# Seeds of a convolution kernel: the factors of the powers as products on GpSimd instead of VectorE

## The chip, the core and the metric

The kernel runs on one core of a Trainium2 chip. A core has TensorE (PE; weight loads are listed apart as PEld), VectorE (DVE), ScalarE (ACT), GpSimd (POOL) and SyncE (SP), which issues the DMAs. Each engine works through its own list of instructions in order; semaphores tie the lists together. The metric is the device time of one execution in microseconds (us); smaller is better.

## The reference, cut to what matters

Two independent halves are computed from fp32 inputs and concatenated: a long convolution (S4D) and an attention with 16 heads.

```python
def _A_ref(u, log_A_real, A_imag, C_real, C_imag, log_dt, D_skip):   # L = 2048, D = 448, N = 256
    dt = jnp.exp(log_dt)
    A = -jnp.exp(log_A_real) + 1j * A_imag
    C = (C_real + 1j * C_imag) * dt[:, None]
    P = jnp.exp((A * dt[:, None])[:, :, None] * pos[None, None, :])
    K = 2.0 * jnp.einsum("dn,dnl->dl", C, P).real
    ...                                     # y = u convolved with K (by FFT of length 2 L)
    return y + u * D_skip[None, None, :]

def _B_ref(x, wqkv, wo):                    # S = 2048, D = 448, H = 16, Dh = 28
    ...                                     # q, k, v = heads of x @ wqkv
    p = _softmax(jnp.einsum("bhqd,bhkd->bhqk", q, k) * Dh ** -0.5, axis=-1)
    return einsum("bhqk,bhkd->bhqd", p, v) ... @ wo
```

## The kernel before

The kernel has two phases.

**The projection phase** (the first 260 us or so) does two things side by side. For the attention it projects x: the 2048 rows come in four chunks `c` of 512. `transposes(c)` turns a chunk on TensorE into four PSUM tiles `pt`, which ScalarE rounds into `xh` and DVE subtracts into the low half `xl`. `qk_proj(c, s, g)` then makes a PSUM tile `pm` for K (s = 1) or Q (s = 0) of a group g of four heads from 12 matrix products, and its `evac` splits it: ScalarE writes the high half of `hl`, DVE the low half (and a difference `kb` for c < 2), and SP sends `hl` to memory as `k` or `q`. `v_proj` makes V (`vst`). There are three `pm` tiles, so PE can start a job only when the job three before it is evacuated. K and Q are read back as `khat` and `qhat` before the attention begins; the chunk c = 3 projects V first and then K and Q.

For the convolution, `seeds(o)` makes the starting values for the powers of exp(A dt), for eight groups `o` of 56 channels, in thirteen steps: scale and turn the parameters (`nat`, `pn`, `tr`), phases and their reduction (tile `tri`, three parts `r`, `sn`, `mg` of 128 x 11 x 112, one for each power of two), sines on ScalarE, `sizes` (Exp of `mg`, whose argument is a product of `tr` with `pw` on GpSimd), and then the products of sizes and sines:

- `g_base` on GpSimd: `gz`, and `r` at two powers in place (listed as `tri<-tri` 128x224);
- `factors` (the change): for three powers at a time, `mg*r` and `mg*sn` into the part `zz` of the tile `sg`, then negative copies by ScalarE (`sg<-sg`). It is called as `fa` and `fb`, two products of 128x336 each, so four for a group;
- `e_base` on GpSimd: six products 128x112 into the tile `qhat` (its place serves as the seeds' e tile), listed as `qhat<-tri`;
- `e3` on DVE: the third power from these (`qhat<-qhat`, `px<-qhat`, `qhat<-qhat,px`);
- `e5` on GpSimd: six operations of 128x336 (`qhat<-qhat`, `x_e<-qhat`, `qhat<-qhat,x_e`);
- `g_first` on DVE: the first powers of g (`sg`, `px`), then copies by ScalarE.

`sg` and the e tile go to memory (`sd`). The tiles `tri` and `sg` have two buffers, the e tile three.

The steps of the seeds and the jobs of the projection are written out in slots: four slots for each group, with the jobs spread over 37 slots. In this phase the order that results on each engine is not the program's: the tile framework's scheduler places the instructions when the kernel is built. Where two engines are called with the same step, the order therefore can change in other places as well.

At the end of the phase the row maxima of the first block are taken (DVE reads `pm` and `pt`).

**The attention phase** keeps the program's order on every engine: for 256 steps, scores (`pss`), Exp on ScalarE (`p`), the product with V (`po`), and between them the maxima of later blocks, the powers of the convolution (`e` on GpSimd, `g` on DVE), its transforms and the output.

All instructions are recorded with the line of one helper (L75), so they are told apart by their tiles.

Of the kernel before, what the change touches and what calls it, by code (L numbers as in the profile page):

```python
# [90 lines left out]
def body(ctx, tc, a, out):  # L91
# [120 lines left out]
    with ExitStack() as st:  # L212
# [98 lines left out]
        mul = lambda e, o_, x_, y_: e.tensor_tensor(o_, x_, y_, ALU.mult)  # L311

        def seeds(o):

            q = {}
            vec, pol, act = nc.vector, nc.gpsimd, nc.scalar
# [3 lines left out]
            vk = lambda t, k: t[:, k:k + 3, :].rearrange("p k (b h) -> p k b h", h=16)  # L320
# [79 lines left out]

            def factors(i, k, p_, n_):
                zz, mg = q["zz"], q["mg"]
                mul(vec, zz[:, i:i + 3, :, 0, :], vk(mg, k), vk(q["r"], k))
                mul(vec, zz[:, i:i + 3, :, p_, :], vk(mg, k), vk(q["sn"], k))
                for k in range(i, i + 3):
                    act.activation(zz[:, k, :, n_, :], zz[:, k, :, p_, :], AF.Copy, scale=-1.0)

# [19 lines left out]
            def load():  # L427
                if o not in nats:
                    load_nat(o)
                q["nat"] = nats.pop(o)  # L430
            dts = lambda *r: [lambda i=i: times_dt(i) for i in r]
            fa, fb = lambda: factors(0, 3, 2, 1), lambda: factors(3, 8, 1, 2)
            return [[load], [exp_a] + dts(1, 2, 3), dts(0), [turn], [phases], [reduce], [sines], [sizes, g_base],
                    [places, fa, e_base], [e3, g_first], [fb, e5, g_copies], [put_g], [put_e]]
# [695 lines left out]
```

## Time and profile before

| | us |
|---|---|
| three runs before | 1300.53, 1301.88, 1303.57 |
| median of the runs | 1301.88 |
| profiled execution, span from first to last instruction | 1301.1 |

A time of the profiled execution beyond its span is not given; the runs lie 0.6 below to 2.5 above that span, and their median 0.8 above it.

| engine | busy us | share of the span |
|---|---|---|
| PE | 1228.2 | 94% |
| ACT | 952.4 | 73% |
| DVE | 948.0 | 73% |
| POOL | 871.1 | 67% |

The profile is one execution. An instruction's row has its start, its duration, engine, operation, output and inputs with their shapes, and in brackets how long the engine stood idle before it and which instruction ended that wait. Idle time of an engine that is not on the way to the end costs nothing. A duration includes time in which the instruction had begun but was held up.

### The profile page before, as it was taken

Reading aid. Unit: us, or ns where it says so; the run is one execution under the profiler, and the core shown is the slowest. Engines: PE = TensorE matmul, PEld = TensorE weight load, DVE = VectorE, ACT = ScalarE, POOL = GpSimd, SP = SyncE. Lnnn points to the kernel's source line nnn. Section 1 sums busy time; section 2 is a strip of 40 time slices with the busy share of each in tenths; the row PEclk is TensorE's granted clock in tenths of the full one; section 3 lists DMA queues with packets and bytes.
Section 4 is the critical chain, followed back from the end, with each engine's and each line's share of the span. In section 5 each row is a group of like instructions: output and inputs, shape, how many; then the busy total and the mean of one; then the engine's idle time right before and its main releaser. Section 6 shows DMA issues by size and latency. Waiting matters only on the chain.

```text
span 1301.1 us, 33177 instructions
## 1 busy us (share of the span) xinstructions
PE 1228.2 (94%) x12625; PEld 701.0 (54%) x12625; DVE 948.0 (73%) x2106; ACT 952.4 (73%) x2068; POOL 871.1 (67%) x736
## 2 busy tenths in 40 slices
PE   6878985899999999999999999999999999999997
PEld 5657763355555555555555555555555555544433
DVE  5887896987777887787788888888888655645111
ACT  4775763488888888888888888888887766756552
POOL 3676683298888878888869999998996212424421
PEclk9888997999999999999999999999999999999999
DMA  6677769835866555458644131733425453647656
GB/s 194 203 258 244 249 206 294 237 77 124 195 137 149 124 146 148 140 147 231 181 126 96 54 95 32 182 91 83 103 51 148 153 158 133 201 144 244 198 162 174
DMA packets 200088, 205.35 MB, mean 158 GB/s; under 512 B 95993, under 2 KB 158521, under 8 KB 197881
## 3 DMA queue, kind: packets, MB, share of 16 engines
q1 hardware_dynamic: 199928, 203.23, 56.2%
q8 instruction: 100, 1.64, 0.5%
q14 instruction: 60, 0.48, 0.1%
HBM read 120.73 MB, written 82.18 MB: 156 GB/s over the span
## 4 chain that ended last, share of the span: by engine, by line
PE 71%; DVE 10%; DMA 6%; POOL 5%; ACT 3%; issue 3%; SPq 0%; POOLq 0%; ACTq 0%; DVEq 0%
PE pm L75 40%; PE pss L75 16%; PE po L75 15%; DVE tri L75 2%; DVE mx L75 2%; POOL e L75 1%; POOL qhat L75 1%; DMA k<-hl 1%; ACT tri L75 1%; DVE qhat L75 1%; DVE sg L75 1%; DMA tri<-in_B_wqkv 1%; DVE px L75 1%; DMA khat<-k 1%; DMA ut<-in_A_u 1%
## 5 line engine op out<-in xcount | busy, mean ns | idle before, releaser
L75 ACT ACTIVATE p<-pss 128x512 f32<-128x512 f32 x1024 | 560.9, 609 | 111.6 <-PE pss L75 108.6
L75 PE MATMUL pss<-qhat,khat 128*128 128x512 f32 x1024 | 402.5, 399 | 1.5 <-ACT p L75 1.4
L75 DVE TENSOR_REDUCE mx<-pm 128x1 f32<-128x512 f32 x500 | 321.4, 684 | 109.2 <-PE pm L75 107.1
L75 PE MATMUL pm<-khat,qhat 128*128 128x512 f32 x749 | 326.3, 438 | 3.4 <-DVE mx L75 2.1
L75 POOL TENSOR_TENSOR e<-e,sdb 128x256 f32<-128x256 f32 x168 | 202.0, 1202 | 116.2 <-ACT e L75 61.2
L75 PE MATMUL po<-p,v 128*32 128x512 f32 x2048 | 269.1, 594 | 0.0
L75 POOL TENSOR_TENSOR e<-e,eu 128x256 f32<-128x256 f32 x168 | 248.4, 1478 | 13.2
L75 PEld LDWEIGHTS pm<-khat,qhat 128*128 128x128 f32 x749 | 141.0, 189 | 199.7 <-ACT p L75 47.8
L75 DVE CUSTOM_DVE_ANT_0 rl<-pm,rl 128x512 f32<-128x512 f32 x249 | 171.4, 688 | 65.2 <-ACT rl L75 61.5
L75 PEld LDWEIGHTS pss<-qhat,khat 128*128 128x128 f32 x1024 | 190.2, 188 | 45.7 <-issue 10.8
L75 POOL TENSOR_TENSOR eu<-e,sdb 128x256 f32<-128x256 f32 x168 | 202.2, 1203 | 0.0
L75 POOL TENSOR_TENSOR p<-pr,pr 64x448 f32<-64x448 f32 x64 | 73.3, 1145 | 158.5 <-PE pm L75 133.2
L75 ACT ACTIVATE rl<-pm 128x512 f32<-128x512 f32 x249 | 150.8, 606 | 20.4 <-PE pm L75 20.4
L75 DVE TENSOR_TENSOR g<-g,zg 128x128 f32<-128x128 f32 x392 | 162.1, 413 | 3.4
L75 PE MATMUL pm<-xh,khat 112*128 112x512 f32 x256 | 94.1, 451 | 23.2 <-DVE hl L75 11.1
L75 PE MATMUL pm<-kdif,qhat 128*128 128x512 f32 x249 | 100.5, 404 | 2.6 <-DMA v<-v 1.3
L75 DVE TENSOR_TENSOR zg<-g,zg 128x128 f32<-128x128 f32 x224 | 88.0, 393 | 5.0
L75 PEld LDWEIGHTS pm<-e,g 128*32 128x32 f32 x3584 | 57.2, 109 | 43.8 <-issue 16.1
L75 DVE TENSOR_TENSOR pr<-pm,ub 128x448 f32<-128x448 f32 x64 | 37.0, 619 | 56.4 <-PE pm L75 42.0
L75 PEld LDWEIGHTS pm<-xh,khat 112*128 112x128 f32 x256 | 54.2, 217 | 39.4 <-DVE hl L75 12.9
L75 PE MATMUL pm<-e,g 128*32 128x64 f32 x3584 | 73.0, 222 | 1.9 <-POOL e L75 1.9
L75 ACT ACTIVATE y<-pm 128x448 f32<-128x448 f32 x48 | 26.5, 553 | 58.2 <-PE pm L75 33.8
(134 smaller groups left out, 1470.3 us busy)
## 6 DMA issues: line engine op xcount, KB each, us to landing
sdb<-sd SPq DMA_DIRECT2D x56, 336.0 KB
khat<-k SPq DMA_DIRECT2D x64, 256.0 KB
qhat<-q SPq DMA_DIRECT2D x64, 256.0 KB
sd<-sg SPq DMA_DIRECT2D x8, 1456.0 KB
k<-hl SPq DMA_DIRECT2D x16, 512.0 KB
q<-hl SPq DMA_DIRECT2D x16, 512.0 KB
mw<-in_mw SPq DMA_DIRECT2D x16, 512.0 KB
sd<-qhat SPq DMA_DIRECT2D x8, 896.0 KB
```

The lines of the kernel that those rows point to most:

```text
L75: i = f(*args, **kw)
```

## The change

The two products of `factors` are issued to GpSimd instead of DVE. Thus 32 products of 128x336 (four for each of eight groups) change the engine; the operands, the copies on ScalarE that follow, and all else in the source stay the same. The order in which the scheduler places the other instructions of the projection phase changes in some places.

```diff
             def factors(i, k, p_, n_):
                 zz, mg = q["zz"], q["mg"]
-                mul(vec, zz[:, i:i + 3, :, 0, :], vk(mg, k), vk(q["r"], k))
-                mul(vec, zz[:, i:i + 3, :, p_, :], vk(mg, k), vk(q["sn"], k))
+                mul(pol, zz[:, i:i + 3, :, 0, :], vk(mg, k), vk(q["r"], k))
+                mul(pol, zz[:, i:i + 3, :, p_, :], vk(mg, k), vk(q["sn"], k))
                 for k in range(i, i + 3):
                     act.activation(zz[:, k, :, n_, :], zz[:, k, :, p_, :], AF.Copy, scale=-1.0)
```

In the changed order of group 2 and 3 (found from the two programs' lists), GpSimd has group 2's four products between group 2's bases, and three of group 3's before the second half of group 3's bases; group 3's `gz` now comes before those bases and no longer after them. DVE has the first `xl` of c = 2, and ScalarE the second `xh`, behind all of group 3's `g_first`; before, five operations of `g_first` came after the first `xl`. On DVE, group 2's first `sg<-pn,tri` (a step of `g_first`) now stands ahead of the evacuation `hl` of the next K job; before, it stood behind two evacuations. At the end of the phase the order of SP's DMAs is the same but for single places.

## The prediction

> **What bounds the kernel now.** I read the page, then the busy time by stretch, the waits of TensorE, the chain that ended last, and last how the change reorders the instructions of each engine.
>
> ```profile
> span 1301.1 us, 33177 instructions
> ```
> ```profile
> 30.00:212.00 182.00, 144.04 (x628) 115.87 (x628) 149.98 (x249) 125.19 (x250) 126.42 (x137) 0.88 0.71 237
> 212.00:238.00 26.00, 20.18 (x49) 10.06 (x49) 21.38 (x48) 7.77 (x13) 0.00 (x0) 0.84 1.05 266
> 262.00:1301.00 1039.00, 1022.95 (x11806) 550.18 (x11804) 740.31 (x1720) 794.34 (x1756) 727.70 (x571) 1.00 0.52 138
> ```
> After each stretch and its length stand the busy us of PE, PEld, DVE, ACT and POOL, the granted clock, the DMA share and GB/s. From 262 us PE is busy for 98.5% of the time, and nothing there is changed: that part moves as a whole. The moved products lie in 30 to 212 us, where no engine is full: PE 144 of 182, DVE 150, POOL 126. Waits set its length.
>
> ```profile
> PE pm L75 <- DVE hl L75: 13.2, 6, 5.4
> PE pm L75 <- DVE kb L75: 6.8, 4, 4.3
> PE pt L75 <- DVE xl L75: 6.1, 4, 2.8
> PE pm L75 <- ACT vst L75: 2.8, 1, 2.8
> ```
> ```profile
> 201.61 6.66 DMA q<-hl
> 208.33 12.53 DMA k<-hl
> 220.88 10.06 DMA khat<-k
> ```
> The first fence has what TensorE waited for in that stretch (total, times, longest): 26.1 us (13.2 + 6.8 + 6.1) for evacuations of PSUM on DVE. The second is the chain behind it: the last K and Q go to memory and come back, with the DMA engines full (share 1.05). So a delay of the last evacuations reaches the end nearly one for one, and DVE's queue is what TensorE waits for. That speaks for relieving DVE; the question is what DVE's queue itself waits for.
>
> **The moved instructions.** 32 products 128x336, four for each group o of the seeds.
>
> ```profile
> L75 DVE TENSOR_TENSOR sg<-tri 128x336 f32<-128x336 f32 x32 | 21.7, 684 | 6.3 <-ACT tri L75 6.1
> ```
> ```profile
> L75 DVE TENSOR_TENSOR sg<-tri x32: 490/510/1171, 39.1 to 196.7; 128x336 f32<-128x336 f32 x32
> L75 POOL TENSOR_TENSOR qhat<-tri x48: 418/434/1624, 40.1 to 198.7; 128x112 f32<-128x112 f32 x48
> L75 POOL TENSOR_TENSOR x_e<-qhat x16: 1016/1022/2220, 52.8 to 205.6; 128x336 f32<-128x336 f32 x16
> L75 POOL TENSOR_TENSOR tri<-tr,pw x8: 2244/2249/3445, 31.1 to 181.4; 128x1232 f32<-128x1232 f32 x8
> ```
> The last rows give shortest, median and longest ns. DVE loses 21.7 us (32 x 684 ns). No row shows this product on POOL. The same size there (x_e) takes 1.02 us; a line through 112 and 1232 elements (434 and 2249 ns) gives 0.80 us at 336. I take 1.02, the row of the same size and kind, with 0.80 and, for neighbours' waits, 1.3 as ends (684/510 = 1.34 is how far waiting stretched the same products on DVE). POOL gains 33 us (26 to 42) and stands at 159 of 182 us (152 to 168). The table of the Trainium skill, GPSIMD Engine Reference, 3.1 Elementwise, has POOL 1.96 times slower than DVE for this operation; as an estimate from 490 ns that is 0.96 us, and the sum below would be 0.5 us smaller. No DMA is moved.
>
> **Where it lands.** A mean of 159 hides the dense places.
>
> ```profile
> 77.00:118.00 41.00, 27.77 (x104) 22.38 (x103) 36.47 (x60) 29.74 (x63) 32.08 (x36) 0.79 0.62 215
> 118.00:160.00 42.00, 38.81 (x187) 31.53 (x185) 32.14 (x48) 28.82 (x52) 21.92 (x28) 0.96 0.76 255
> 160.00:208.00 48.00, 36.46 (x146) 28.85 (x145) 39.68 (x70) 29.19 (x60) 39.31 (x39) 0.88 0.74 232
> ```
> In 77 to 118 us groups 2 and 3 follow each other without a pause: eight products more make 32.1 + 8.2 = 40.3 of 41 us, so POOL becomes full there, while it still has 20 us idle in the next stretch.
>
> Step 1, Exp behind POOL's product of exponents:
> ```profile
> 77.02 3.44 POOL L75 TENSOR_TENSOR tri<-tr,pw 128x1232 f32<-128x1232 f32 x1
> ...
> 80.50 1.23 ACT L75 ACTIVATE tri<-tri 128x1232 f32<-128x1232 f32 x1 [2.79 <-POOL tri L75]
> ...
> 83.00 1.22 PE L75 MATMUL pm<-xh,khat 112*128 112x512 f32 x2 [5.38 <-DVE hl L75]
> ```
> POOL makes group 2's exponents only after group 1; ACT's Exp waits for them; the next evacuation stands behind Exp in ACT's queue, DVE's half of it behind ACT's, and PE waits 5.38 us. Group 1's last two factor products now come ahead on POOL: 2 x 1.02 = 2.0 us later; its other two fit into waits of POOL.
>
> Step 2, the 3rd power behind POOL's bases:
> ```profile
> 89.69 2.65 POOL L75 TENSOR_TENSOR qhat<-tri 128x112 f32<-128x112 f32 x3
> ...
> 93.03 1.77 POOL L75 TENSOR_TENSOR qhat<-tri 128x112 f32<-128x112 f32 x3
> 95.81 0.81 POOL L75 TENSOR_TENSOR dhl<-kb,dhl 128x256 fp32r<-128x256 f32 x1 [1.01 <-POOL qhat L75]
> 97.26 1.02 POOL L75 TENSOR_TENSOR qhat<-qhat 128x336 f32<-128x336 f32 x1 [0.65 <-DVE qhat L75]
> ...
> 108.44 0.81 POOL L75 TENSOR_TENSOR gz<-tri 128x224 f32<-128x224 f32 x1
> ```
> ```profile
> 107.29 0.58 DVE L75 TENSOR_TENSOR qhat<-qhat 128x112 f32<-128x112 f32 x1 [1.92 <-POOL qhat L75]
> ...
> 113.20 0.68 DVE L75 TENSOR_TENSOR xl<-pt,xh 112x512 fp32r<-112x512 f32 x1
> ...
> 113.94 0.43 PE L75 MATMUL pt<-ident,xn 128*112 128x128 f32 x2 [2.58 <-DVE xl L75]
> ```
> DVE's third power of group 3 already waits 1.92 us for POOL. Behind it in DVE's queue stand the first powers of g and then xl, the low half of the next 512 rows of x, for which PE waits 2.58 us: all of c = 2 hangs on it. In the changed order seven moved products and group 3's gz (0.81) come ahead of those bases: 7 x 1.02 + 0.81 = 7.9 us. Back come about 1.8 us, by which group 2's bases were stretched (2.65 + 1.77 against 6 x 0.434), and 1.7 us of POOL's waits (1.01 + 0.65), which its later work fills. Net 7.9 + 2.0 - 3.5 = 6.4 us.
>
> Step 3: the order also puts xl, and ACT's xh, behind the whole of group 3's first powers; before, five of those operations came after the first xl. The first and the last of the five:
> ```profile
> 114.76 0.39 DVE L75 TENSOR_TENSOR px<-pn,gz 128x224 f32<-128x224 f32 x1
> ...
> 117.82 0.55 DVE L75 TENSOR_TENSOR sg<-sg,px 128x224 f32<-128x224 f32 x1
> ```
> Five at about 0.5 us are 2.5; the moved product that stood ahead of xl is gone (0.7): 1.8 us. The start of c = 2 moves by 6.4 + 1.8 = 8.2 us. By the ends of the product, nine of them (two in step 1, seven in step 2) make it 6.2 at 0.80 and 10.7 at 1.3.
>
> Step 4: from 118 to 160 PE is busy 38.8 of 42 us, so it cannot catch up, while POOL can. In 160 to 208 POOL gets nine products, 9.2 us on 39.3 of 48, and DVE loses nine, 9 x 0.684 = 6.2 us: full against relieved. I take nothing for it, with -6.2 (all of DVE's relief on the path) to +3.4 (39.3 + 9 x 1.3 over 48, and a start without slack) as its ends. The chain of DMAs then follows the last evacuations; one of them already waits for a DMA:
>
> ```profile
> 205.01 0.69 ACT L75 ACTIVATE hl<-pm,kones 128x512 fp32r<-128x512 f32 x1 [5.88 <-DMA k<-hl]
> ```
> That wait could swallow up to 5.9 us of lateness if the DMAs kept their pace, but the DMAs are fed by the same late evacuations, so I take off nothing.
>
> Sum: 1301.1 + 8.2 = 1309.3 us of span. The median of the three runs (1301.9) lies 0.8 above the span: 1310.1, said as 1310.
>
> **Rivals.** *Faster: DVE's relief decides.* TensorE's 26.1 us of waits on DVE shrink with DVE's load, by 21.7 of 150 us or 14%: 3.8 us, 1301.9 - 3.8 = 1298. For it: DVE is the fuller engine and ends most of PE's waits. Against it: at two of the longest, POOL stands behind DVE (steps 1 and 2). It decides if group 3's third power still starts by about 107 us. Chance 0.18.
>
> *The lateness is absorbed.* POOL's waits for ACT's sines are longer than the additions, and the wait of 5.88 us for the DMA takes most of the rest: 8.2 - 5.9 = 2.3, or 1304. Chance 0.12.
>
> *One engine at a time.* Neighbours stretch each other:
>
> ```profile
> 163.88 3.53 POOL L75 TENSOR_TENSOR qhat<-qhat 128x336 f32<-128x336 f32 x1 [0.94 <-DVE tri L75]
> ```
> ```profile
> 164.07 1.44 DVE L75 TENSOR_TENSOR tri<-tri,pw 128x1232 f32<-128x1232 f32 x1
> ```
> A product that takes 1.02 us alone took 3.53 beside DVE's. If one always excludes the other and their common time fills the phase, the moved work costs what it claims: 32 x (1.02 - 0.49) = 17 us, 1301.9 + 17 = 1319. Against it, both still have idle time together in 118 to 160. Chance 0.14. The Trainium skill, SBUF — State Buffer, SBUF: two separate sides, says why: DVE with two inputs in SBUF and a GpSimd instruction take turns on one port pair, for the whole instruction, so these products keep excluding the other engine wherever they run.
>
> **How the numbers follow.** About 0.2% (2.6 us) is what a measurement of this kernel can tell from no change. The forecast (slower, 1306 to 1313) has 0.56, the one-at-a-time rival 0.14: slower 0.70. Absorbed 0.12 counts as the same, relief 0.18 as faster. The range reaches from just under the relief rival, 1297, to the port rival, 1319; it leaves out larger gains, up to DVE's whole 21.7 us, and larger losses.
>
> **What would show it.** In the profile of the changed kernel: the moved product on POOL near 1.02 us (0.80 to 1.3); POOL near 159 us in the phase; the Exp of group 2 starting near 82.5; DVE's third power of group 3 near 113.5, waiting for POOL several us; c = 2's first xl near 121; the chain of DMAs as before, some 8 us later; from there to the end as long as before. A third power near 107 us, or PE's waits on DVE falling below 22 us, would make the forecast wrong.

## The result, and the profile after

The changed kernel is slower: 1316.25 us (median of four runs, 1315.51 to 1316.94). Against the kernel before on the same chip the ratio is 1.0106, with a 95% interval of 1.0087 to 1.0126, or +13.8 us (1% of 1302 us is 13.0 us); the interval is 11.3 to 16.4 us. The forecast was +8.2: the sign and the place were right, the size was too small. The time lies above the 1306 to 1313 that had the largest chance, and below the 1319 of the one-at-a-time rival.

Busy time by stretch in the kernel after, with the columns of the prediction:

```profile
span 1315.2 us, 33183 instructions
```
```profile
77.00:127.00 50.00, 31.22 (x116) 24.82 (x116) 32.54 (x55) 29.95 (x65) 39.51 (x48) 0.79 0.53 182
127.00:170.00 43.00, 38.89 (x180) 31.53 (x178) 26.52 (x39) 26.46 (x46) 22.36 (x29) 0.93 0.73 245
170.00:222.00 52.00, 37.39 (x154) 28.90 (x152) 35.99 (x64) 31.28 (x63) 46.49 (x52) 0.90 0.73 230
276.00:1315.00 1039.00, 1023.11 (x11807) 550.56 (x11806) 741.04 (x1721) 793.86 (x1757) 726.75 (x571) 1.00 0.51 138
```

From 276 us on everything takes 1039 us, as it did from 262 us before: the attention is only 14 us later. All of the loss lies in the projection phase: the stretches of 41, 42 and 48 us are now 50, 43 and 52 us long. The second of these matters, too, because there the forecast took no loss; TensorE's granted clock there (the share of its full clock that the profile shows as granted) is 0.93, where it was 0.96.

What TensorE waited for, from 30 to 225 us (total, times, longest):

```profile
PE pm L75 <- DVE hl L75: 22.7, 7, 6.7
PE pt L75 <- DVE xl L75: 8.5, 5, 2.8
PE pm L75 <- ACT vst L75: 5.3, 3, 3.8
PE pm L75 <- DVE kb L75: 3.0, 3, 1.3
```

The waits on DVE are 34.2 us, after 26.1, although DVE was relieved of 32 products. With ScalarE's part TensorE waited 39.7 us, after 28.9: 10.8 us more, which is most of the loss but not all. TensorE itself also took longer, 146.80 us for 620 matmuls in the phase, where it was 144.04 us for 628 before.

So the question is what DVE did with its time. What DVE waited for from GpSimd in the same stretch, first in the kernel before, then after:

```profile
DVE qhat L75 <- POOL qhat L75: 3.4, 4, 1.9
DVE sg L75 <- POOL tri L75: 2.2, 4, 0.6
DVE px L75 <- POOL qhat L75: 1.4, 3, 0.7
```
```profile
DVE px L75 <- POOL qhat L75: 13.9, 6, 5.1
DVE qhat L75 <- POOL qhat L75: 10.1, 5, 6.4
DVE sg L75 <- POOL tri L75: 7.7, 5, 2.7
```

Before, DVE waited 7.0 us for GpSimd; after, 31.7. The 24.7 us more are about what DVE lost in busy time, 27.9 us (158.35 and 130.46 us in that stretch):

```profile
30.00:225.00 195.00, 153.32 (x651) 121.48 (x651) 158.35 (x268) 128.78 (x256) 126.42 (x137) 0.87 0.74 240
```
```profile
30.00:225.00 195.00, 146.80 (x620) 116.84 (x620) 130.46 (x217) 123.81 (x249) 145.11 (x169) 0.87 0.67 221
```

(Part of the 27.9 is work of the attention that began before 225 us in the kernel before, and not yet in the one after.) DVE gave work away and then stood still for GpSimd's results, ahead of the evacuations that stand behind them in its queue. ScalarE's waits for GpSimd rose in the same way, from 10.8 to 26.0 us.

### The profile page after: what moved, and what is told of

The parts are those of the page before. It is cut to its first block, busy times and chain, and to the rows that moved or that the text cites. A ratio compares the mean times of both kernels' runs of the same rounds, so it can differ in the third digit from the quotient of the medians.

```text
span 1315.2 us, 33183 instructions
## 1 busy us (share of the span) xinstructions
PE 1232.4 (94%) x12625; PEld 703.7 (54%) x12625; DVE 929.6 (71%) x2074; ACT 950.5 (72%) x2068; POOL 889.1 (68%) x768
## 4 chain that ended last, share of the span: by engine, by line
PE 73%; POOL 9%; DVE 7%; ACT 4%; issue 3%; DMA 2%; SPq 1%; POOLq 0%; ACTq 0%; DVEq 0%
PE pm L75 41%; PE pss L75 16%; PE po L75 15%; POOL qhat L75 3%; DVE mx L75 2%; POOL sg L75 2%; POOL e L75 1%; POOL tri L75 1%; DVE rl L75 1%; ACT tri L75 1%; DMA khat<-k 1%; PE pt L75 1%; DVE qhat L75 1%; POOL x_e L75 1%; POOL p L75 1%
## 5 line engine op out<-in xcount | busy, mean ns | idle before, releaser
L75 POOL TENSOR_TENSOR e<-e,eu 128x256 f32<-128x256 f32 x168 | 248.1, 1477 | 13.2
L75 PEld LDWEIGHTS pss<-qhat,khat 128*128 128x128 f32 x1024 | 190.7, 189 | 45.8 <-issue 10.8
L75 PE MATMUL pm<-xh,khat 112*128 112x512 f32 x256 | 93.0, 446 | 21.6 <-DVE hl L75 15.8
```

The lines of the kernel that those rows point to most:

```text
L75: i = f(*args, **kw)
```

## The experiments

Two theories were at stake. **In-order theory:** every engine works strictly in order, so a result that GpSimd makes later also delays all that stands behind its reader on DVE or ScalarE, evacuations above all. **Price theory** (the port rival): each moved product costs the difference of its two durations, or a share of time in which only one of the two engines can work, wherever it stands. Differences in us below are the ratio against the kernel before on the same chip times 1302.

### One pair of groups at a time

Four kernels move only the products of two groups: 0 and 1, 2 and 3, 4 and 5, 6 and 7.

```diff
-                mul(vec, zz[:, i:i + 3, :, 0, :], vk(mg, k), vk(q["r"], k))
-                mul(vec, zz[:, i:i + 3, :, p_, :], vk(mg, k), vk(q["sn"], k))
+                mul(pol if o in (0, 1) else vec, zz[:, i:i + 3, :, 0, :], vk(mg, k), vk(q["r"], k))
+                mul(pol if o in (0, 1) else vec, zz[:, i:i + 3, :, p_, :], vk(mg, k), vk(q["sn"], k))
```

> Only groups 0 and 1 (8 of the 32 products) go to GpSimd. Queue theory (the loss comes where DVE's and ScalarE's queues stand behind GpSimd's bases at two places, group 3 ahead of the next rows of x and group 6 ahead of the first K of c = 3): only step 1's lateness of the Exp of group 2, +1 to +3 us. Port theory (every product costs its extra turn of a port that DVE and GpSimd share, wherever it is moved): 8 x 0.47 = +3.8 us, as the full change's 15 us over 32.

> Only groups 2 and 3 go to GpSimd, the dense place before c = 2. Queue theory: the start of c = 2 comes 6 to 8 us later (DVE's third power of group 3 waits for GpSimd, the low half of x stands behind it), and the end +6 to +8 us, half of the full change's loss with a quarter of the products. Port theory: +3.8 us.

> Only groups 4 and 5 go to GpSimd, where it has waits of 5 to 6 us in each group. Queue theory: the waits take them in, 0 us, from -3 (DVE relieved) to +2. Port theory: +3.8 us.

> Only groups 6 and 7 go to GpSimd. Queue theory: the first evacuation of K of c = 3 stands behind the third power of group 6 in DVE's order and waits for GpSimd: +4 to +6 us, the second part of the full change's loss. Port theory: +3.8 us; this one alone does not tell the two apart, the four together do (even, or 2 / 7 / 0 / 5).

| groups moved | us | ratio, 95% interval | difference, us |
|---|---|---|---|
| 0 and 1 | 1311.13 | 1.0061 (1.0048 to 1.0074) | +7.9 |
| 2 and 3 | 1307.24 | 1.0027 (1.0017 to 1.0037) | +3.5 |
| 4 and 5 | 1303.99 | 1.0001 (0.9992 to 1.0011) | +0.1 |
| 6 and 7 | 1307.03 | 1.0025 (1.0014 to 1.0036) | +3.3 |

The four add up to 14.8, close to the 13.8 of the whole change, but they are far from even. An even price per product is refuted: eight products cost nothing in groups 4 and 5 and 7.9 us in groups 0 and 1. Of my in-order numbers only that for groups 4 and 5 held: I had put most of the loss on groups 2 and 3 (6 to 8 us, 3.5 measured) and 1 to 3 us on groups 0 and 1 (7.9 measured), and 6 and 7 stayed below their 4 to 6. TensorE's waits show the places. The kernel with groups 0 and 1 moved:

```profile
86.14 2.08 PE L75 MATMUL pm<-xh,khat 112*128 112x512 f32 x4 [6.72 <-DVE hl L75]
...
118.78 1.96 PE L75 MATMUL pt<-ident,xn 128*112 128x128 f32 x8 [4.50 <-DVE xl L75]
```
```profile
156.27 0.74 PE L75 MATMUL pm<-vh,xh 112*128 112x448 f32 x1 [4.42 <-ACT vst L75]
```

With groups 4 and 5, and with 6 and 7 moved:

```profile
112.64 1.91 PE L75 MATMUL pt<-ident,xn 128*112 128x128 f32 x8 [2.57 <-DVE xl L75]
```
```profile
191.20 0.92 PE L75 MATMUL pm<-xh,khat 112*128 112x512 f32 x2 [3.98 <-DVE hl L75]
```

Groups 0 and 1 alone bring the lateness of step 1 (83.00 before) and 4.8 us of the 8.5 at the start of c = 2, though none of group 2's or 3's products is moved: the queue of GpSimd hands its lateness from group to group, and DVE's order of this kernel also has `xl` behind more of group 3's `g_first`. Groups 6 and 7 alone make the K evacuation late that step 4 had passed over. Groups 4 and 5 add no such wait of TensorE, and cost nothing. Yet DVE's own waits for GpSimd rise the most there: 15.3 us, against 10.5, 12.6 and 12.2 us in the other three kernels (in the order of the table) and 7.0 before. So the sum of these waits is no measure of the cost; it matters what stands behind each of them.

Waits are not the whole loss here either. In the kernel with groups 2 and 3 moved TensorE waited only 0.5 us more than before up to the attention, but its matmuls of the phase took 147.2 us in all, where they took 144.0; in 120 to 160 us its granted clock was 0.91, and 0.96 before. Each kernel has one profile, so it isn't shown that the moved products make the clock lower.

### Load alone, relief alone

`load`: the products stay on DVE, and GpSimd makes the same products once more into a tile that nobody reads (the operands are the same; the place written to is another). `relief`: the products are left out, and ScalarE copies one operand in their place.

```diff
                 mul(vec, zz[:, i:i + 3, :, p_, :], vk(mg, k), vk(q["sn"], k))
+                zx = s_p.tile([128, 3, NH], F32, name="zx")
+                mul(pol, zx, mg[:, k:k + 3, :], q["r"][:, k:k + 3, :])
+                mul(pol, zx, mg[:, k:k + 3, :], q["sn"][:, k:k + 3, :])
```
```diff
-                mul(vec, zz[:, i:i + 3, :, 0, :], vk(mg, k), vk(q["r"], k))
-                mul(vec, zz[:, i:i + 3, :, p_, :], vk(mg, k), vk(q["sn"], k))
+                act.activation(zz[:, i:i + 3, :, 0, :], vk(q["r"], k), AF.Copy)
+                act.activation(zz[:, i:i + 3, :, p_, :], vk(q["sn"], k), AF.Copy)
```

> The factors stay on DVE, and GpSimd makes the same 32 products once more into a tile that nobody reads (work added, none moved). The order of DVE's instructions stays that of the kernel before. Queue theory (DVE and ScalarE stand behind GpSimd's lateness): +10 to +18 us, all of the full change's loss or a little more, since DVE is not relieved. Order theory (the loss is the new order of the evacuations): at most +4. Port theory: 32 x 0.92 = +29 us.

> No factor products at all: ScalarE copies the sines in place of them (32 copies of 128x336, about 14 us in all; the product with the sizes is left out). DVE loses 21.7 us, GpSimd gains nothing. It prices DVE's relief alone: -2 to -6 us by the relief rival's 3.8; about 0 if DVE's share of those waits is only waiting for others; above 0 if ScalarE, which stands ahead of the evacuations too, takes its place.

`load`: 1323.77 us, ratio 1.0157 (1.0139 to 1.0176), +20.4 us, between the 10 to 18 of the in-order theory and the 29 of the port theory. Nobody reads these products, and the orders of DVE, ScalarE and TensorE in this phase are those of before, so neither a new reader nor a new order explains this: it is GpSimd's later queue, or the time that the two engines take from each other. TensorE's waits on DVE in `load`:

```profile
88.43 2.07 PE L75 MATMUL pm<-xh,khat 112*128 112x512 f32 x4 [8.34 <-DVE hl L75]
...
125.42 1.96 PE L75 MATMUL pt<-ident,xn 128*112 128x128 f32 x8 [8.80 <-DVE xl L75]
```

The same two instructions started at 83.00 and 113.94 before: +5.4 and +11.5 us, at exactly the places of steps 1 and 2. But the whole kernel's DVE busy time also rises, from 948.0 to 959.0 us, with no work added to DVE. Since DVE's list is the same in both kernels, its lateness can be added up instruction by instruction. The last evacuation starts 18.5 us later (at 210.79 and 229.34 us): 10.1 us of this are DVE instructions that took longer, 7.9 us are longer waits for GpSimd's bases, and the rest is 0.5 us. So both theories have a part in `load`. The third power of group 3, which took 0.58 us after a wait of 1.92 before, shows both at once:

```profile
115.62 3.80 DVE L75 TENSOR_TENSOR qhat<-qhat 128x112 f32<-128x112 f32 x1 [4.72 <-POOL qhat L75]
```

GpSimd was busy for 3.59 of these 3.80 us.

The full change costs 6.6 us less than `load`. That is the order of what DVE's relief is worth here, if the two add up, which no run shows; it is more than the 3.8 of the relief rival, and a third of the load's cost.

`relief` was meant to show this directly and failed: 1309.73 us, ratio 1.0045 (1.0029 to 1.0060), +5.9. The 32 copies (13.7 us on ScalarE) stand ahead of ScalarE's halves of the evacuations, and DVE waits for those:

```profile
DVE hl L75 <- ACT hl L75: 26.8, 12, 6.3
```

It was 16.6 us before. The work took the same toll from another queue, so nothing follows for DVE's relief.

### GpSimd made lighter

`beforex` and `afterx` are the two kernels with GpSimd's largest product, that of the exponents, replaced: Exp of ScalarE takes its powers of two as its scale.

```diff
-                mul(pol, mg, lb(q["tr"]), kb)
...
-                act.activation(q["mg"], q["mg"], AF.Exp)
+                for k in range(LV):
+                    act.activation(q["mg"][:, k, :], q["tr"], AF.Exp, scale=2.0 ** k)
```

> The kernel before, but the exponents: instead of GpSimd's product 128x1232 and one Exp, ScalarE takes Exp of the row times 2^k, eleven times 128x112. GpSimd loses 8 x 2.42 = 19 us, ScalarE gains about 8 x (11 x 0.29 - 1.23) = 16 us. Queue theory: PE's wait of 5.38 us behind Exp, and so behind GpSimd, goes: -3 to -6 us. If ScalarE's own load sets the pace: +3 to +10.

> The full change with the exponents on ScalarE as in the kernel named beforex. Queue theory: with GpSimd 19 us lighter and Exp no longer behind it, the move costs 0 to +6 us against beforex. Port theory: the products take their turns all the same, +12 to +17 against beforex.

| | us | ratio, 95% interval | difference, us |
|---|---|---|---|
| `beforex` | 1295.12 | 0.9935 (0.9917 to 0.9953) | -8.5 |
| `afterx` | 1309.93 | 1.0045 (1.0029 to 1.0061) | +5.9 |

`beforex` beats both kernels, by more than the 3 to 6 us that were expected. The step in which ScalarE's Exp waited for GpSimd (step 1) is gone, though ScalarE now waits 9.7 us for GpSimd's `gz`, and DVE's two large operations on `tri`, 1886 and 1847 ns each in the kernel before, are held up less; in `beforex`:

```profile
L75 DVE TENSOR_TENSOR tri<-tri,pw 128x1232 f32<-128x1232 f32 x8 | 12.8, 1595 | 0.0
L75 DVE TENSOR_TENSOR tri<-tri 128x1232 f32<-128x1232 f32 x8 | 12.7, 1589 | 0.1
```

But the change costs the same on top of it, 5.9 + 8.5 = 14.4 us, where the in-order theory had expected 6 at most, since GpSimd is back at 127.0 us in the phase, as before the change (126.4). That number was wrong, and the 12 to 17 us of the port theory held. What my version of the theory lacked: it isn't enough that GpSimd's total is that of the kernel before. (Against its own control `beforex`, which has 104.6 us, it rose by 22.4 us.) Of DVE's waits for GpSimd, those of the third power, in `beforex` and in `afterx`:

```profile
DVE px L75 <- POOL qhat L75: 1.9, 2, 1.2
```
```profile
DVE px L75 <- POOL qhat L75: 11.7, 4, 5.0
```

All of them together were 12.9 us and became 28.5: the waits are there again, at other places.

### The moved products last

In the last four kernels the first half of each group's products is issued two stages later (the expectation counts one stage, and four products where there are two), in the program behind the bases and the third power. In `late` they are on GpSimd, in its control `latev` on DVE; `latex` and `latevx` are the same two with the exponents on ScalarE. The order that the scheduler made of it does not put them last, as the traces show: in `late`, seven of the eight groups have two products behind the first three bases and ahead of `tri<-tri` and the other three bases, and two behind all the bases and ahead of `e5`; in the last group all four stand ahead of the bases. In `latex` three groups have all four behind their bases. So these kernels test another place of the products, not the last.

```diff
-                    [places, fa, e_base], [e3, g_first], [fb, e5, g_copies], [put_g], [put_e]]
+                    [places, e_base], [e3, g_first], [e5, fa, fb, g_copies], [put_g], [put_e]]
```

> The changed kernel with one more edit: in each group the first four moved products are put one stage later, so that GpSimd gets the bases first and the moved products last of all (they are wanted only by the store of the group). All 32 products stay on GpSimd, so its work and its use of memory are those of the changed kernel. In-order theory (DVE and ScalarE, each working strictly in order, stand behind GpSimd's results, which the moved products make late): DVE's waits for GpSimd in 30 to 225 us fall from 31.7 us to 8 to 18, and the time to 1302 to 1309 us, so at least half of the +14.5 is gone. Price theory (each product costs its 0.5 us of difference, or a share of DVE's turn at memory, wherever it stands): 1314 to 1318, as the changed kernel.

> The same stage order as the run with the moved products last, but with all 32 products left on DVE: the kernel before with its first four products of each group one stage later. It is the control for the edit of the stage order. In-order theory: DVE now does the products behind its first third powers and g factors, DVE is the engine with most to do, so 1298 to 1306 us; the difference to the run with the products on GpSimd is then 0 to 6 us. Price theory: the difference is 13 to 16 us.

> Moved products on GpSimd and put last in their group, and GpSimd's product of exponents replaced by eleven Exp on ScalarE: GpSimd's work in 30 to 225 us falls from 147.9 us (products last) to about 127, that of the kernel before (126.4), with DVE still relieved of its 16 us. In-order theory with GpSimd's total as the cause: with the load gone, the waits of DVE for GpSimd fall from 22.8 us to about 10 and the run stands within 5 us of its control (the same kernel with the products on DVE), near 1293 to 1302 us. Price theory (the place and GpSimd's total do not matter): 12 to 16 us above the control. A third way: DVE's waits stay at 20 us or more though GpSimd's total is that of before, and the run is 6 to 12 us above the control: then it is the chain of each group (the moved products between a base and the one who needs it), not the total.

> Control of the run with the products last and the exponents on ScalarE: all products on DVE, exponents on ScalarE, the stage order of the products-last kernels. In-order theory and price theory alike: GpSimd has only about 105 us of work, and the time is that of the kernel before with the exponents on ScalarE plus the 3 us that the stage order cost with the exponents on GpSimd, so 1296 to 1301 us.

| | us | ratio, 95% interval | difference, us |
|---|---|---|---|
| `late` | 1314.58 | 1.0077 (1.0055 to 1.0098) | +10.0 |
| `latev` | 1307.49 | 1.0025 (1.0012 to 1.0037) | +3.3 |
| `latex` | 1309.39 | 1.0036 (1.0021 to 1.0050) | +4.7 |
| `latevx` | 1297.59 | 0.9945 (0.9930 to 0.9960) | -7.2 |

With the exponents on GpSimd, the later stage halves the price of the engine: `late` less `latev` is 6.8 us, where the change as it stands has 13.8. Neither theory's number for that difference holds. (The 1314.58 us lies in the price theory's 1314 to 1318, but the kernel before took 1305.18 on that chip.) DVE's wait for the bases falls (px and qhat 24.0 to 8.5 us), but its waits for the `tri<-tri` of `g_base`, which still stands behind two of its group's products, rise from 7.7 to 14.3 us. With the exponents on ScalarE it is the third way of the expectation: `latex` less `latevx` is 11.9 us, at a GpSimd that is no busier than before the change (125.9 us, but 105.4 in `latevx`). DVE's waits for GpSimd in `latex`, then in `latevx`:

```profile
DVE sg L75 <- POOL tri L75: 23.4, 7, 6.8
...
DVE px L75 <- POOL qhat L75: 13.5, 6, 4.2
DVE qhat L75 <- POOL qhat L75: 5.1, 6, 2.1
```
```profile
DVE qhat L75 <- POOL qhat L75: 4.7, 4, 3.0
DVE sg L75 <- POOL tri L75: 4.6, 7, 1.2
...
DVE px L75 <- POOL qhat L75: 1.7, 2, 1.0
```

42.0 us against 11.0. The longest of these waits is that of group 3's `g_first`:

```profile
127.51 0.56 DVE L75 TENSOR_TENSOR sg<-pn,tri 128x224 f32<-128x224 f32 x1 [6.82 <-POOL tri L75]
127.91 0.72 DVE L75 SCALAR_TENSOR_TENSOR hl<-pm,kones,hl 128x512 fp32r<-128x512 f32 x1
```

GpSimd made what it reads (`tri<-tri` of `g_base`) at 126.81 us, straight behind the six operations of group 3's `e5` (from 118.83) and two of its moved products (1.79 us), without a pause; and an evacuation of K stands behind the wait.

### What the runs settle, and what they don't

In all four pairs (products on DVE, products on GpSimd) the kernel gets slower by 6.8 to 14.4 us, and DVE's waits for GpSimd rise: 7.0 to 31.7, 12.9 to 28.5, 7.4 to 22.8 and 11.0 to 42.0 us. They don't rise in step with the cost, which is 13.8, 14.4, 6.8 and 11.9 us. An even price per product is out (0.1 us for groups 4 and 5). That GpSimd's total is too high is out in so far as the cost stays when the total is that of the kernel before (`afterx`, `latex`). A new order alone isn't it (`load` keeps the order and loses more); how much of the change's own loss is its new order isn't shown.

The one-at-a-time rival is not out. Take the time in which GpSimd or a DVE product with two operands in SBUF was running, over 30 to 208 us before and 30 to 222 after. The time with both of them, in which one can hold up the other, fell from 51.7 to 36.5 us, since DVE had fewer such products. But the time with at least one of them rose from 143.1 to 158.9 us, by 15.8, and the time with neither hardly changed (34.9 and 33.1 us). That is close to the 17 us which the rival reckons with. Added up in the same way, the time with at least one rises by 15 to 16 us in all four pairs, while the cost is 6.8 us in one and 14.4 in another, and by 2.8 us with groups 4 and 5 moved, at no cost. So the added time of the two engines is there each time, and how much of it the kernel pays depends on the place.

What stays open: no kernel had the products on GpSimd and the waits gone, so that the waits are the cause is read from the traces, not shown by removing them. `load` could be parted into waits and held-up DVE instructions; the change can't, because DVE's order differs. Why TensorE's clock was lower in parts of the slower kernels stays open as well.

## Why the prediction was right or wrong

**The moved product** was taken at 1.02 us, with 0.80 and 1.3 as ends. The products on GpSimd, in the listing by tile and in the groups:

```profile
L75 POOL TENSOR_TENSOR sg<-tri x32: 895/922/2107, 39.1 to 211.0; 128x336 f32<-128x336 f32 x32
```
```profile
L75 POOL TENSOR_TENSOR sg<-tri 128x336 f32<-128x336 f32 x32 | 31.9, 1001 | 0.0
```

The mean of 1.00 us agrees with the 1.02. Its median is 0.92, near the 0.96 that was estimated from the Trainium skill, GPSIMD Engine Reference, 3.1 Elementwise: 922/510 is 1.81 times DVE's, where the page has 1.96 for an add of 2048 elements. The trace agrees within a tenth.

**GpSimd near 159 us in the phase** was wrong: 145.11 in the longer phase. The added 31.9 us are there, but GpSimd's other work became shorter, since fewer of DVE's products held it up: its whole busy time rose by 18.0 us (871.1 to 889.1) only. The gain of 33 us was mis-sized, though not the lateness at the critical place, because there GpSimd really was full: from group 2's first moved product at 92.52 to the third power at 113.87 us it was busy for 20.66 of 21.35 us.

**Step 1** (Exp of group 2 behind GpSimd) was right in its mechanism:

```profile
80.50 2.80 POOL L75 TENSOR_TENSOR tri<-tr,pw 128x1232 f32<-128x1232 f32 x1
83.34 1.23 ACT L75 ACTIVATE tri<-tri 128x1232 f32<-128x1232 f32 x1 [5.17 <-POOL tri L75]
...
85.83 2.07 PE L75 MATMUL pm<-xh,khat 112*128 112x512 f32 x4 [6.72 <-DVE hl L75]
```

Exp started 2.84 us later than before (2.0 forecast), and TensorE 2.83 us later with it: the delay passes through ScalarE's queue and DVE's one for one.

**Steps 2 and 3** were right in their times, to 0.7 us:

```profile
113.87 1.40 DVE L75 TENSOR_TENSOR qhat<-qhat 128x112 f32<-128x112 f32 x1 [6.39 <-POOL qhat L75]
...
121.21 0.56 DVE L75 TENSOR_TENSOR sg<-sg,px 128x224 f32<-128x224 f32 x1
121.68 0.68 DVE L75 TENSOR_TENSOR xl<-pt,xh 112x512 fp32r<-112x512 f32 x1
```
```profile
122.42 0.65 PE L75 MATMUL pt<-ident,xn 128*112 128x128 f32 x4 [1.88 <-DVE xl L75]
```

The third power was forecast at 113.5 and waited 6.39 us for GpSimd; `xl` was forecast at 121 and came at 121.68; TensorE began c = 2 8.5 us later than before, with 8.2 forecast. The sum up to there is what the prediction said it would be. How it is made up is not shown, and in part the agreement looks like luck. With groups 0 and 1 alone c = 2 began 4.8 us late, where step 1 had 2.0; with groups 2 and 3 alone it began 3.7 us late (at 117.64), where steps 2 and 3 had 6.2. The two misses are in opposite directions, and 4.8 + 3.7 is 8.5 again.

**Step 4 failed.** It took nothing for 118 to 208 us, with -6.2 to +3.4 as ends, on the balance of busy times. (The upper end adds up to 3.0, as 39.3 + 9 x 1.3 - 48; the rest, for a start without slack, comes from no row.) In truth the lateness grew by 4.9, from 8.5 to 13.4 us: the last evacuation of the phase moved from 210.79 to 224.19. The larger part, 3.2 us, arose between the start of c = 2 and the first K job behind the V jobs of c = 3, before and after:

```profile
113.94:168.60 54.66, 51.16 (x240) 42.30 (x241) 44.52 (x67) 38.52 (x72) 32.52 (x35) 0.94 0.81 269
```
```profile
122.42:180.33 57.91, 52.95 (x241) 43.21 (x241) 37.88 (x57) 36.12 (x68) 34.34 (x40) 0.91 0.76 254
```

The same 240 matmuls (a matmul from before the stretch reaches into the second row) kept TensorE busy for 52.95 us instead of 51.16, at a granted clock of 0.91 instead of 0.94: 1.8 us, for which the prediction had no term. TensorE's idle time grew by 1.5 us. One of its waits is of the kind of step 1, in the stretch that I had called full for TensorE:

```profile
156.88 2.25 POOL L75 TENSOR_TENSOR tri<-tr,pw 128x1232 f32<-128x1232 f32 x1
```
```profile
159.17 1.23 ACT L75 ACTIVATE tri<-tri 128x1232 f32<-128x1232 f32 x1 [3.67 <-POOL tri L75]
160.31 0.58 ACT L75 ACTIVATE hl<-pm 128x512 fp32r<-128x512 f32 x1
160.78 0.97 ACT L75 ACTIVATE vst<-pm 128x448 f32<-128x448 f32 x2
```
```profile
161.37 0.47 PE L75 MATMUL pm<-vh,xh 112*128 112x448 f32 x1 [1.16 <-ACT vst L75]
```

An Exp waits for GpSimd's product of exponents, and an evacuation of Q and two of V stand behind it on ScalarE. The same Exp had waited 3.01 us in the kernel before, so the place isn't new, and its wait grew by 0.7 us only. By the next K job the lateness of TensorE was 11.7 us (168.60 before, 180.33 after). The other 1.7 us came with the K and Q jobs that follow, where the third power stands in the way again, now with an evacuation of K behind it in DVE's changed order:

```profile
191.84 1.53 DVE L75 TENSOR_TENSOR qhat<-qhat 128x112 f32<-128x112 f32 x2 [1.06 <-POOL qhat L75]
193.29 0.74 DVE L75 SCALAR_TENSOR_TENSOR hl<-pm,kones,hl 128x512 fp32r<-128x512 f32 x1
```
```profile
194.09 0.73 PE L75 MATMUL pm<-xh,khat 112*128 112x512 f32 x2 [4.25 <-DVE hl L75]
```

I had followed GpSimd's readers instruction by instruction up to 118 us and then weighed busy times, and a balance of busy times doesn't show who stands behind a wait, nor a lower clock.

**The DMA tail** was right: nothing was swallowed. TensorE began the attention at 228.02 us, after 214.87, 13.2 us later, about as late as the last evacuation; the wait of 5.88 us for the DMA is still 5.30.

**The rivals.** *Relief decides* fell: the third power was not near 107 us, and TensorE's waits on DVE rose above 26 us. DVE's relief may still be worth something (6.6 us by `load`, if the two add up), but `relief` didn't show it. *The lateness is absorbed* fell with the DMA tail. *One engine at a time* came nearest to the time, with 1319, and its sum of 17 us fits the 15.8 us by which the time with at least one of the two at work grew. As it was put it fell short: their common time doesn't fill the phase (33.1 us had neither), and two pairs of groups differed by 7.8 us for the same work. What the Trainium skill says in SBUF — State Buffer, SBUF: two separate sides, of the shared pair of ports agrees with the durations here: as DVE's products left, GpSimd's were held up less (511 to 436 ns, below).

## What to carry to other kernels

Before moving work to an engine with idle time, list who reads that engine's results, and what stands behind each reader in its own queue; follow this to the end of the phase, not only where the engine looks full. Evening out busy times helps nothing when the relieved engine then waits for the loaded one. It paid to do the opposite, to take from GpSimd a product that ScalarE gets as the scale of its Exp, though that makes eleven Exp out of one: -8.5 us.

## What the runs showed of the hardware that was not expected

DVE and GpSimd hold each other up so much that moving work between them changes the work that stays. GpSimd's 128x112 products, before and after:

```profile
L75 POOL TENSOR_TENSOR qhat<-tri 128x112 f32<-128x112 f32 x48 | 23.0, 511 | 0.0
```
```profile
L75 POOL TENSOR_TENSOR qhat<-tri 128x112 f32<-128x112 f32 x48 | 19.3, 436 | 0.0
```

They got 15% shorter when DVE's products left. In `load`, where products were only added, DVE's third power of one group was held up for 3.2 us. The busy times of the two engines together are the same (1819.1 us before, 1818.7 after), though a product takes 1.00 us on GpSimd and took 0.68 on DVE.
